# Gate sums of an mLSTM and MoE kernel: chunks 1 to 4 on 128 partitions by 128 columns, chunk 5 by itself over units 5 to 8

## The chip, the cores and the metric

The kernel runs on one core of one Trainium2 chip, as one launch. The metric is the device time of that launch in microseconds. TensorE is called PE here, VectorE DVE, ScalarE ACT, GpSimd POOL, and SyncE, which only issues DMAs in this kernel, SP.

## The reference

An mLSTM recurrence over 768 steps for 4 batches of 8 heads (head size 40), and behind it a mixture of 16 experts on the 3072 tokens that it yields. The parts that matter here are the two gates and what is derived from them:

```python
for t in range(S):                                   # S = 768
    m_new = np.maximum(f_gate[:, :, t] + m, i_gate[:, :, t])
    f_stab = np.exp(f_gate[:, :, t] + m - m_new)
    i_stab = np.exp(i_gate[:, :, t] - m_new)
    m = m_new
    C = f_stab * C + i_stab * np.einsum('bhd,bhe->bhde', vt, kt)
    n = f_stab * n + i_stab * kt
    h_tilde = np.einsum('bhde,bhe->bhd', C, qt)
    y[:, :, t] = o * h_tilde / np.maximum(np.abs(nq), 1.0)   # nq = n . q
```

Then `x = y` as 3072 rows of 320, a softmax over 4 groups and over 4 experts of the chosen group picks one expert for each token, and that expert computes `relu(x @ w1) @ w2`, weighted.

## The kernel before, in words

The sequence is cut into 6 chunks of 128 steps. A chunk of one batch is a **unit**: unit u is chunk u // 4 of batch u % 4, so units 0 to 3 are chunk 0, units 4 to 7 chunk 1, and units 20 to 23 chunk 5. Within a chunk the recurrence is written as an attention: the scores (`scores`, line 205, tile `sp`), multiplied by a decay matrix `ab` into `pt` (`masked`, line 210), times the values (`values`, line 277, tile `av`), and a state `Cflat` is carried from chunk to chunk (`carried`, line 230; `state`, line 249).

The decay matrix comes from the **gate sums**, which is what is changed. For each of the 32 heads, one running maximum M of the gates (a scan over time, line 873), the step of the decay Dl = f + M(t-1) - M(t) (lines 877 and 878), its sum A within the chunk (a scan, line 880), and i - M - A (lines 875 and 881, kept in `G`). A is split into three bf16 pieces, which stand below each other in `Apc` (32 rows each, lines 884 to 889). `aprod` (line 178) spreads them over the partitions with a matmul, and `exps` (line 188) makes `ab` from that, with a bias per column, `bcol`. `bcol`, and two more small tables with `eacol` and `decs`, come from transposes of `G` and `A_` on PE (lines 896 and 898), copied out of the accumulator by DVE (line 904), and from one matmul on the last columns of `Apc`, masked into `ends` (lines 907 and 911).

All of it is done on 32 partitions, one for each head, in three pieces that `sums` holds as generators: `gate_sums(0, P)` for chunk 0 ahead of unit 0, `gate_sums(P, 2 * P)` for chunk 1 during units 0 and 1, and `gate_sums(2 * P, S)` for chunks 2 to 5, 512 columns wide, during units 2 to 4. `sum_on(n)` advances the piece in hand by n steps (up to a `yield`), and that sets where its instructions stand in the queues. The table `(0, 0, 3, 2, 9)[u]` says how many steps follow unit u.

Up to unit 21 the order on each engine is the order in which the code is written (`tc.manual_schedule()`). A unit (`unit(u)`) issues the loads of unit u + 3 on SP, the scores of u on PE, then on DVE the normalizing of unit u - 1 (`norm1`, lines 283 to 288, and `rows`, line 293, tile `xn`), on POOL its last product (`rows2`, line 299, tile `x`), on SP the store of it to `x_d`, then `masked`, the first half of `decay(u + 2)`, the transposes of x of unit u - 1 (`turn`, line 307), `values(u)`, `state(u)` and the second half of `decay(u + 2)`. So `decay(4)`, the first unit of chunk 1, stands in unit 2, and `decay(8)`, the first of chunk 2, in unit 6. From unit 5 on the routing of tokens (`route`, lines 374 to 443) runs between units, in steps as well (`go_on`). `first_rows`, called in unit 5, fills a tile with the constants that two later steps write out as rows (lines 467 to 480); it takes a tile of the pool `wst`, which is opened once the gate tiles are given back (`gctx.close()`).

Of the kernel before, what the change touches and what calls it, by code (L numbers as in the profile page):

```python
# [58 lines left out]
def lstm_moe(ctx: ExitStack, tc: tile.TileContext, gates, qkT, nat, og, wcat, w1, w2, cst, out):  # L59
# [809 lines left out]
    def gate_sums(lo, hi):  # L869
        fg, ig = G[:, 0, lo:hi], G[:, 1, lo:hi]  # L870
        q = nc.gpsimd if lo == 0 else nc.vector
        init = NEG if lo == 0 else M_[:, lo - 1:lo]
        nc.vector.tensor_tensor_scan(M_[:, lo:hi], fg, ig, init, op0=ALU.add, op1=ALU.max)
# [3 lines left out]
        nc.vector.tensor_tensor(Dl[:, l1:hi], G[:, 0, l1:hi], M_[:, l1 - 1:hi - 1], op=ALU.add)
# [3 lines left out]
        q.tensor_tensor(Cg[:, lo:hi], Cg[:, lo:hi], A_[:, lo:hi], op=ALU.subtract)
        yield
        p0, r1, p1 = Apc[0:32, lo:hi], Dl[:, lo:hi], A1[:, lo:hi]
        nc.vector.tensor_copy(p0, A_[:, lo:hi])
        nc.vector.tensor_tensor(r1, A_[:, lo:hi], p0, op=ALU.subtract)
# [2 lines left out]
        nc.vector.tensor_tensor(Apc[64:96, lo:hi], r1, p1, op=ALU.subtract)
# [5 lines left out]
        for i in range(n):
            s = slice((cl + i) * P, (cl + i + 1) * P)
            nc.tensor.transpose(out=tp[:, 32 * i:32 * i + 32], in_=Cg[:, s], identity=ident[0:32, 0:32])
            if lo:
                nc.tensor.transpose(out=tp[:, 32 * (n + i):32 * (n + i) + 32], in_=A_[:, s], identity=ident[0:32, 0:32])
        if not lo:
            nc.vector.tensor_copy(bcol[:, 0, :], tp[:, 0:32])  # L900
            return
        w = 32 * n
        both = gp.tile([P, 2, 4 * B * H], F32, name="both")
        nc.vector.tensor_copy(both[:, :, 0:w], tp[:, 0:2 * w].rearrange("p (a w) -> p a w", a=2))
        yield
        ends = gp.tile([P, 4, B * H], BF16, name="ends")
        nc.vector.tensor_tensor(ends[:, 0:n], bc(Apc.rearrange("p (c t) -> p c t", t=P)[:, cl:ch, P - 1:P], (P, n, B * H)),
# [285 lines left out]
```

## Time and profile before

| | |
|---|---|
| three runs | 412.26, 410.71 and 407.75 us, median 410.71 us |
| profiled execution | 411.12 us, of which the span of the profile is 409.5 us |
| mean granted TensorE clock | 0.972 of full speed |
| PE busy | 387.6 us, 95% of the span |
| DVE, ACT, POOL busy | 263.9, 213.4 and 173.9 us |
| bytes by DMA | 83.38 MB, mean 204 GB/s |

The attention takes about the first 160 us of the span, the experts the rest. A row of the timeline starts with the time from the start of the span and the busy time, both in us; what stands in brackets at its end is the idle time of the engine before it and what ended that. A row of a table by stretches gives, for each engine, the busy time and the number of instructions, then the granted clock (PEclk), the share of the 16 DMA engines and GB/s.

### The profile page before, as it was taken

The numbers are of one execution on the slowest core, as the hardware profiler recorded it, in microseconds if no ns is written. First come the engines' busy times: TensorE is split into PE (matmuls) and PEld (weight loads), VectorE is DVE, ScalarE is ACT, GpSimd is POOL, SyncE is SP. The second block draws the span as 40 slices with busy tenths as digits, with TensorE's granted clock in tenths as the row PEclk, the third lists the DMA queues.
The fourth block names the chain that finished last, engine by engine and source line by source line (L and its number), as shares of the span: only waits on it lengthen the run. The fifth ranks groups of instructions, "written<-read, shape, count | busy, mean of one in ns | idle before, by whom it ended". The sixth has DMA issues, their size and how long they took to land.

```text
span 409.5 us, 9797 instructions
## 1 busy us (share of the span) xinstructions
PE 387.6 (95%) x3665; PEld 361.1 (88%) x3665; DVE 263.9 (64%) x692; ACT 213.4 (52%) x541; POOL 173.9 (42%) x232
## 2 busy tenths in 40 slices
PE   7869999999899888899999999999999999999994
PEld 4769898989778777699899999999999999999994
DVE  5695786858979795683966565765845655433530
ACT  5753555654657540534855564755745645443531
POOL 6334467666656463528524234243042325331300
PEclk9987999999999989599999999999999999999998
DMA  7934649988799953418996647676764267786700
GB/s 228 323 118 132 167 139 189 257 186 173 173 241 277 224 140 103 108 27 267 408 398 238 199 175 269 219 239 187 280 219 147 61 242 257 300 304 225 277 20 10
DMA packets 28260, 83.38 MB, mean 204 GB/s; under 512 B 11447, under 2 KB 15406, under 8 KB 24628
## 3 DMA queue, kind: packets, MB, share of 16 engines
q1 hardware_dynamic: 22756, 64.74, 53.5%
q0 software_dynamic: 5232, 17.65, 12.4%
q8 instruction: 29, 0.48, 0.5%
q10 hardware_dynamic: 224, 0.35, 0.4%
q14 instruction: 19, 0.16, 0.2%
HBM read 72.97 MB, written 9.99 MB: 203 GB/s over the span
## 4 chain that ended last, share of the span: by engine, by line
PE 69%; DMA 10%; issue 9%; DVE 5%; POOL 3%; ACT 2%; POOLq 1%; SPq 0%; ACTq 0%; DVEq 0%
PE psh L749 12%; PE av L277 9%; PE psh L717 6%; PE po L770 6%; PE po L772 6%; PE po L771 6%; PE sp L205 4%; PE it L230 3%; DMA w2s<-in_w_dram 3%; DMA x_d<-x 3%; PE it L249 2%; PE po L776 2%; PE aw L178 2%; PE tpm L307 2%; PE po L775 2%
## 5 line engine op out<-in xcount | busy, mean ns | idle before, releaser
L188 ACT ACTIVATE ab<-aw,bcol 128x128 f32<-128x128 f32 x192 | 54.5, 370 | 44.1 <-PE aw L178 43.9
L583 POOL DMA_INDIRECT out_dram<-y,ix x32 | 36.9, 1154 | 78.6 <-ACT y L782 71.3
L770 PE MATMUL po<-w2h,hh 128*128 128x320 f32 (+3 forms) x200 | 63.2, 316 | 0.9 <-ACT hh L703 0.9
L772 PE MATMUL po<-w2h,hh 128*128 128x320 f32 (+3 forms) x200 | 61.8, 309 | 0.0
L771 PE MATMUL po<-w2l,hh 128*128 128x320 f32 (+3 forms) x200 | 61.7, 309 | 0.0
L579 POOL DMA_INDIRECT xg<-x_d,ix x32 | 34.8, 1086 | 55.2 <-DMA ix<-itab 29.0
L642 DVE TENSOR_TENSOR w2l<-w2s,w2h 128x640 fp32r<-128x640 f32 x64 | 50.4, 815 | 10.6 <-ACT w2h L640 10.6
L277 PE MATMUL av<-nt,pt 128*128 128x128 f32 x384 | 50.5, 287 | 1.7 <-DVE pt L210 1.7
L277 PEld LDWEIGHTS av<-nt,pt 128*128 128x128 f32 x384 | 47.9, 202 | 2.3 <-DVE pt L210 1.9
L706 DVE SCALAR_TENSOR_TENSOR hh<-psh,hh 128x256 fp32r<-128x256 f32 (+4 forms) x108 | 35.9, 365 | 17.7 <-ACT hh L703 17.2
L703 ACT ACTIVATE hh<-psh 128x288 fp32r<-128x288 f32 (+8 forms) x68 | 30.2, 443 | 29.5 <-PE psh L749 15.0
L640 ACT CAST w2h<-w2s 128x640 fp32r<-128x640 f32 x64 | 43.2, 724 | 0.0
L717 PE MATMUL psh<-xhl,w1s 128*128 128x144 f32 (+3 forms) x336 | 41.3, 283 | 0.0
L717 PEld LDWEIGHTS psh<-xhl,w1s 128*128 128x128 f32 x336 | 40.9, 191 | 0.1
L782 ACT ACTIVATE y<-po,xg 128x320 f32<-128x320 f32 (+3 forms) x25 | 13.2, 527 | 52.1 <-PE po L772 49.7
L749 PE MATMUL psh<-xhl,w1h 128*128 128x256 f32 (+5 forms) x224 | 38.5, 294 | 0.5 <-ACT xhl L684 0.4
L210 DVE TENSOR_TENSOR pt<-sp,ab 128x512 f32<-128x512 f32 x48 | 30.9, 684 | 10.8 <-PE sp L205 9.6
L770 PEld LDWEIGHTS po<-w2h,hh 128*128 128x128 f32 (+3 forms) x200 | 36.4, 182 | 1.2 <-ACT hh L703 1.2
L772 PEld LDWEIGHTS po<-w2h,hh 128*128 128x128 f32 (+3 forms) x200 | 36.4, 182 | 0.1
L771 PEld LDWEIGHTS po<-w2l,hh 128*128 128x128 f32 (+3 forms) x200 | 36.5, 182 | 0.0
L749 PEld LDWEIGHTS psh<-xhl,w1h 128*128 128x128 f32 x224 | 32.3, 195 | 1.2 <-ACT xhl L684 0.5
L486 POOL DMA_INDIRECT itab<-tokid,slot x24 | 25.9, 1080 | 15.3 <-DVE slot L420 4.3
(195 smaller groups left out, 782.1 us busy)
## 6 DMA issues: line engine op xcount, KB each, us to landing
w1s<-in_w_dram SPq DMA_DIRECT2D x12, 1536.0 KB, 6.8
w2s<-in_w_dram SPq DMA_DIRECT2D x12, 1280.0 KB, 6.3
nt<-in_nat_dram SPq DMA_DIRECT2D x24, 324.0 KB, 6.6
qk<-in_qkT_dram SPq DMA_DIRECT2D x24, 320.0 KB, 6.1
x_d<-x SPq DMA_DIRECT2D x24, 192.0 KB, 4.5
sig<-in_og_dram SPq DMA_DIRECT2D x6, 640.0 KB, 8.1
w1s<-in_w_dram SPq DMA_DIRECT2D x4, 768.0 KB, 11.3
w1s<-in_w_dram POOLq DMA_DIRECT2D x2, 1536.0 KB, 9.1
```

The costliest lines, as they stand in the source:

```text
L188: rt["exp"] = nc.scalar.activation(st_[u]["ab"][:, r, j, :], aw[:, j, :], AF.Exp, bias=bcol[:, c, i:i + 1])
L277: ins = mm(av[:, i:i + P], t["pm"][r][:, pr, :], nt[:, o:o + P], start=True, stop=True)
L579: return nc.gpsimd.indirect_dma_start(out=o, out_offset=None, in_=src, in_offset=bass.IndirectOffsetOnAxis(ap=idx, axis=0))
L583: return nc.gpsimd.indirect_dma_start(out=out, out_offset=bass.IndirectOffsetOnAxis(ap=idx, axis=0), in_=y, in_offset=None, bounds_check=N ...
L640: nc.scalar.copy(a, src[:, s])
L642: lows.append(lambda: nc.vector.tensor_tensor(o[rows], src[rows, s], a[rows].bitcast(F32), op=ALU.subtract))
L706: nc.vector.scalar_tensor_tensor(hh[:, f:f + per, dst], src[:, :, t], 0.0, hr.bitcast(F32)[:, :, t], op0=ALU.max, op1=ALU.subtract)
L717: ins = mm(ps[:, g * W:(g + 1) * W], w1s[:, s], xhl[:, k, :], start=(k == 0), stop=(k == 2))
L749: ins = mm(ps[:, g * W:(g + 1) * W], w[:, s], x, start=(n == 0), stop=(n == len(todo) - 1))
L770: mm(po[0:m], hh[:, f, t], w2h[:, s], start=st0, stop=False)
L771: mm(po[0:m], hh[:, f, t], w2l[:, s], start=False, stop=False)
L772: ins = mm(po[0:m], hh[:, f, tl], w2h[:, s], start=False, stop=sp0)
```

## The change

The gate tiles get another shape. The inputs of the gates are laid out by chunk and head (192 rows of 2 x 128), so that rows 0 to 31 are chunk 0, rows 32 to 159 chunks 1 to 4, and rows 160 to 191 chunk 5. Chunk 0 is computed as before. Chunks 1 to 4 are one piece, `middle_sums()`, on 128 partitions (32 for each chunk) by 128 columns, where `gate_sums(P, 2 * P)` was: four scans of 32 x 128 for the running maximum, each started from the last column of the one before, which a copy moves to the next 32 partitions; everything else in single instructions of 128 x 128. The three bf16 pieces are made in `pc4`, and since `Apc` wants them on other partitions, 12 DMAs on SP's queue carry them there, one for each chunk and piece. Chunk 5 is `gate_sums(1)`, 32 x 128, taken up after unit 4 and spread over units 5 to 8 by the table `(2, 2, 1, 9)[u - 5]`. The transposes of the middle piece are two of 128 x 128, and `bcol` and `eacol` are read straight from PSUM, without the copy `both`.

```diff
+    post = enter(tc.tile_pool(name="post", bufs=2, reuse_waits="tile"))   # was opened after unit 4
...
-    G = gp.tile([B * H, 2, S], F32, name="G")
...
-    R_ = gp.tile([B * H, S], F32, name="R_")
+    G = gp.tile([BH, 2, 2, P], F32, name="G")
+    G4 = gp.tile([P, 2, P], F32, name="G4")
+    ones4 = gp.tile([P, P], F32, name="ones4")
+    M_ = gp.tile([BH, 2, P + 1], F32, name="M_")
+    M4 = gp.tile([P, P + 1], F32, name="M4")
...
+    pc4 = gp.tile([P, 3, P], BF16, name="pc4")
...
     def first_rows():
-        t = wst.tile([P, 3 * F], F32, name="w1s")
+        t = gp.tile([P, 3 * P + ROW], F32, name="rows0")
...
-    def gate_sums(lo, hi):
+    def gate_sums(g):
+        c = (NCH - 1) * g
+        fg, ig, M, dl, A = G[:, g, 0], G[:, g, 1], M_[:, g], Dl[:, g], A_[:, g]
+        q = nc.vector if g else nc.gpsimd
+        if g:
+            nc.vector.tensor_copy(M[:, 0:1], M4[P - BH:P, P:P + 1])
...                                   # the same steps on one chunk of 32 x 128
+        nc.tensor.transpose(out=tp[:, 0:BH], in_=ig, identity=ident[0:BH, 0:BH])
+        if not g:
+            nc.vector.tensor_copy(bcol[:, 0, :], tp[:, 0:BH])
+            return
+        nc.tensor.transpose(out=tp[:, BH:2 * BH], in_=A, identity=ident[0:BH, 0:BH])
+        yield from columns(tp, c, c + 1)
+
+    def columns(tp, cl, ch):
...                                   # as before, without both: ends and bcol, then the matmul, eacol, decs
+
+    def middle_sums():
+        fg, ig = G4[:, 0], G4[:, 1]
+        for k in range(NCH - 2):
+            rs = slice(k * BH, (k + 1) * BH)
+            nc.vector.tensor_copy(M4[rs, 0:1], M4[(k - 1) * BH:k * BH, P:P + 1] if k else M_[:, 0, P:P + 1])
+            nc.vector.tensor_tensor_scan(M4[rs, 1:P + 1], fg[rs], ig[rs], M4[rs, 0:1], op0=ALU.add, op1=ALU.max)
+            if k % 2:
+                yield
+        nc.vector.tensor_tensor(D4, fg, M4[:, 0:P], op=ALU.add)
+        nc.vector.tensor_tensor(D4, D4, M4[:, 1:P + 1], op=ALU.subtract)
+        yield
+        nc.vector.tensor_tensor_scan(A4, ones4, D4, 0.0, op0=ALU.mult, op1=ALU.add)
+        nc.vector.tensor_copy(pc4[:, 0], A4)
+        yield
+        nc.vector.tensor_tensor(D4, A4, pc4[:, 0], op=ALU.subtract)
+        nc.vector.tensor_copy(pc4[:, 1], D4)
+        nc.vector.tensor_tensor(pc4[:, 2], D4, pc4[:, 1], op=ALU.subtract)
+        for k in range(NCH - 2):
+            for i in range(3):
+                nc.sync.dma_start(Apc[i * BH:(i + 1) * BH, (k + 1) * P:(k + 2) * P], pc4[k * BH:(k + 1) * BH, i])
+        yield
+        nc.vector.tensor_tensor(ig, ig, M4[:, 1:P + 1], op=ALU.subtract)
+        nc.vector.tensor_tensor(ig, ig, A4, op=ALU.subtract)
+        yield
+        tp = ps_1.tile([P, 512], F32, name="tp", tag="tp")
+        nc.tensor.transpose(out=tp[:, 0:P], in_=ig, identity=ident)
+        nc.tensor.transpose(out=tp[:, P:2 * P], in_=A4, identity=ident)
+        yield from columns(tp, 1, NCH - 1)
...
-        sums.append(gate_sums(P, 2 * P))
+        sums.append(middle_sums())
...
         unit(1, first=True)
         sum_on(9)
-        sums.append(gate_sums(2 * P, S))
         for u in range(2, 5):
             unit(u)
-            sum_on((0, 0, 3, 2, 9)[u])
-    gctx.close()
+        sums.append(gate_sums(1))
+        for u in range(5, 9):
+            unit(u)
+            sum_on((2, 2, 1, 9)[u - 5])
     gctx.close()
```

How this moves rows in the queues is shown at three places. The first is SP, from the store of x of unit 0 to that of unit 1. Before:

```order
L314 DMA x_d<-x 128x384
L145 DMA qk_90<-in_qkT_dram 80x1024
L168 DMA nt<-in_nat_dram 128x648
L314 DMA x_d<-x 128x384
L145 DMA qk_91<-in_qkT_dram 80x1024
```

The same place after, where the line numbers are those of the changed file:

```order
L320 DMA x_d<-x 128x384
L941 DMA Apc<-pc_132 32x128 x12
L151 DMA qk_93<-in_qkT_dram 80x1024
L174 DMA nt<-in_nat_dram 128x648
L320 DMA x_d<-x 128x384
```

Twelve DMAs now stand between the store of unit 0 and the loads of unit 5. The kernel's DMAs share eight completion semaphores in turn, so each of them also waits until the DMA eight places ahead of it has landed.

The second place is DVE between the products of unit 1 (`pt`) and the normalizing of unit 1 (`den`). Before:

```order
L210 TENSOR_TENSOR pt<-sp,ab 128x512 x2
L884 CAST Apc<-A__122 32x128
L885 TENSOR_TENSOR Dl<-A__122,Apc 32x128
L887 CAST A_124<-Dl 32x128
L888 TENSOR_TENSOR Apc<-Dl,A_124 32x128
L904 COPY both<-tp 128x2x32
L907 TENSOR_TENSOR ends<-Apc,sel_b 128x32
L909 COPY bcol<-both 128x32
L286 TENSOR_SCALAR den<-av 128x8
```

After (`A_130` is A4, `D_129` is D4, `M_126` is M4, `pc_132` is pc4):

```order
L216 TENSOR_TENSOR pt<-sp,ab 128x512 x2
L933 SCALAR_TENSOR_TENSOR A_130<-ones_124,D_129 128x128
L934 CAST pc_132<-A_130 128x128
L936 TENSOR_TENSOR D_129<-A_130,pc_132 128x128
L937 CAST pc_132<-D_129 128x128
L938 TENSOR_TENSOR pc_132<-D_129,pc_132 128x128
L943 TENSOR_TENSOR G_123<-G_123,M_126 128x128
L944 TENSOR_TENSOR G_123<-G_123,A_130 128x128
L912 TENSOR_TENSOR ends<-Apc,sel_b 128x128
L914 COPY bcol<-tp 128x128
L292 TENSOR_SCALAR den<-av 128x8
```

`ends` reads `Apc`, which DVE and POOL wrote before; now the DMAs write it, and `ends` waits for all twelve. The row behind it is the normalizing of unit 1.

The third place is DVE in unit 2, from its products to those of unit 3. Before:

```order
L210 TENSOR_TENSOR pt<-sp,ab 128x512 x2
L873 SCALAR_TENSOR_TENSOR M__120<-G,M__120 32x512
L875 TENSOR_TENSOR G<-G,M__120 32x512
L877 TENSOR_TENSOR Dl<-G,M__120 32x512
L878 TENSOR_TENSOR Dl<-Dl,M__120 32x512
L880 SCALAR_TENSOR_TENSOR A__122<-R__123,Dl 32x512
L881 TENSOR_TENSOR G<-G,A__122 32x512
L286 TENSOR_SCALAR den<-av 128x8
```

After:

```order
L216 TENSOR_TENSOR pt<-sp,ab 128x512 x2
L292 TENSOR_SCALAR den<-av 128x8
L293 SCALAR_TENSOR_TENSOR den<-av,den 128x8
L294 RECIPROCAL den<-den 128x8
L299 SCALAR_TENSOR_TENSOR xn<-sig,av 128x320
```

The six rows of 512 columns are gone from here, and so are the four of them that stood behind the products of unit 3 and the transposes and copies behind unit 4.

More of the change, by code (lines that the diff above doesn't have):

```diff
@@ L881, in gate_sums @@
[L881 removed]
+        nc.vector.tensor_tensor_scan(A, ones4[0:BH], dl, 0.0, op0=ALU.mult, op1=ALU.add)
+        q.tensor_tensor(ig, ig, A, op=ALU.subtract)
         yield
[L883 to L885 removed]
+        p0, p1 = Apc[0:32, cols], A1[:, g]
+        nc.vector.tensor_copy(p0, A)
@@ L894, in gate_sums @@
[L894 to L907, printed above, removed]
-                                bc(sel_b.unsqueeze(1), (P, n, B * H)), op=ALU.mult)
-        nc.vector.tensor_copy(bcol[:, cl:ch, :].rearrange("p c h -> p (c h)"), both[:, 0, 0:w])
+        nc.tensor.transpose(out=tp[:, 0:BH], in_=ig, identity=ident[0:BH, 0:BH])
@@ new lines, in gate_sums @@
+        if not g:
[4 more added lines that the diff above has]
+    def columns(tp, cl, ch):
+        n = ch - cl
+        w = n * BH
+        ends = gp.tile([P, 4, BH], BF16, name="ends")
+        nc.vector.tensor_tensor(ends[:, 0:n], bc(Apc.rearrange("p (c t) -> p c t", t=P)[:, cl:ch, P - 1:P], (P, n, BH)),
+                                bc(sel_b.unsqueeze(1), (P, n, BH)), op=ALU.mult)
+        nc.vector.tensor_copy(bcol[:, cl:ch, :].rearrange("p c h -> p (c h)"), tp[:, 0:w])
@@ L924, in lstm_moe @@
     with tc.manual_schedule():
-        nc.sync.dma_start(G[:, :, 0:P], gates[:, :, 0:P])
+        nc.sync.dma_start(G[:, 0], gates[0:BH])
         nc.scalar.dma_start(cs, cst)
-        nc.scalar.dma_start(G[:, :, P:], gates[:, :, P:])
+        nc.scalar.dma_start(G4, gates[BH:BH + P])
+        nc.scalar.dma_start(G[:, 1], gates[BH + P:])
         nc.vector.memset(ones_b, 1.0)
@@ L931, in lstm_moe @@
         busy(11)
[L932 to L934 removed]
+        nc.vector.memset(ones4, 1.0)
+        nc.vector.memset(Dl[:, 0, 0:1], 0.0)
         nc.vector.memset(Apc[96:P], 0.0)
@@ L986, in lstm_moe @@
     mxp = enter(tc.tile_pool(name="mxp", bufs=2, reuse_waits="tile"))
-    post = enter(tc.tile_pool(name="post", bufs=2, reuse_waits="tile"))
     pools["ws"] = [wsa]
@@ L991, in lstm_moe @@
     with tc.manual_schedule():
-        for u in range(5, MANUAL):
+        for u in range(9, MANUAL):
             unit(u, 6 if 13 <= u <= 16 else 0)
@@ L1136, in _lay @@
     q, k, v, o = (inputs[n] for n in ('q', 'k', 'v', 'o_gate'))
-    gates = c(np.stack([inputs['f_gate'].reshape(B * H, S), inputs['i_gate'].reshape(B * H, S)], axis=1))
+    gates = np.stack([inputs['f_gate'].reshape(B * H, NCH, P), inputs['i_gate'].reshape(B * H, NCH, P)], axis=2)
+    gates = c(gates.transpose(1, 0, 2, 3).reshape(NCH * B * H, 2, P))
     def tr(a):
```

43 lines of the change are left out of this document (19 added, 24 removed).

## The prediction

> **What bounds the kernel now.** I read the shares of busy time first, then the granted clock, then a table with one stretch for each unit of the attention.
>
> ```profile
> PE 387.6 (95%) x3665; PEld 361.1 (88%) x3665; DVE 263.9 (64%) x692; ACT 213.4 (52%) x541; POOL 173.9 (42%) x232
> PEclk9987999999999989599999999999999999999998
> ```
>
> PE is busy for 95%, so what counts is where PE stands still or runs at a lower clock. The clock falls once early, in the slices from about 20 to 41 us, which are units 2 to 4. The stretches below run from the first scores of one unit to those of the next: units 1, 2, 3, 4, 5, 6, 7, 8 and 9.
>
> ```profile
> 12.47:20.03 7.56, 6.35 (x79) 5.24 (x75) 3.89 (x16) 5.09 (x20) 2.86 (x8) 1.00 1.05 335
> 20.03:24.96 4.93, 4.68 (x60) 4.11 (x60) 4.62 (x10) 2.52 (x11) 1.42 (x2) 1.00 0.57 179
> 24.96:35.27 10.31, 7.34 (x62) 6.57 (x60) 9.02 (x20) 3.97 (x11) 3.89 (x5) 0.68 0.31 86
> 35.27:41.48 6.21, 6.21 (x100) 5.62 (x100) 3.20 (x9) 2.97 (x11) 2.68 (x5) 0.99 0.46 142
> 41.48:49.14 7.66, 7.05 (x87) 6.13 (x86) 5.20 (x16) 3.60 (x14) 3.65 (x6) 1.00 0.65 196
> 49.14:54.95 5.81, 5.81 (x88) 5.41 (x86) 4.49 (x17) 3.05 (x11) 2.92 (x5) 1.00 0.65 186
> 54.95:60.77 5.82, 5.66 (x78) 5.09 (x76) 5.33 (x14) 3.95 (x11) 5.01 (x7) 1.00 0.30 92
> 60.77:67.49 6.72, 6.66 (x103) 5.77 (x101) 4.28 (x13) 3.43 (x13) 4.42 (x8) 1.00 0.81 107
> 67.49:72.90 5.41, 5.41 (x78) 5.02 (x77) 3.83 (x12) 2.50 (x10) 3.63 (x6) 1.00 1.13 258
> ```
>
> Unit 2 takes 4.93 us and unit 3, with the same work on PE, 10.31 us. Unit 5 takes 7.66 us, where its like, unit 9, takes 5.41. Elsewhere PE is full. The timeline and the clock show what happens in unit 3:
>
> ```profile
> 22.50 1.26 DVE L873 TENSOR_TENSOR_SCAN M__120<-G,M__120 32x512 f32<-32x512 f32 x1
> 27.07 0.68 DVE L881 TENSOR_TENSOR G<-G,A__122 32x512 f32<-32x512 f32 x1
> 27.68 0.15 DVE L286 TENSOR_SCALAR den<-av 128x8 f32<-128x8 f32 x1
> 29.47 0.90 PE L307 MATMUL tp<-cs,x 128*128 128x128 f32 x3 [2.83 <-POOL x L299]
> 30.17 3.62 PE L277 MATMUL av<-nt,pt 128*128 128x128 f32 x16
> 28.00:28.50 0.50, 0.00 (x0) 0.00 (x0) 0.47 (x3) 0.00 (x0) 0.00 (x0) 1.00 0.00 0
> 28.50:29.00 0.50, 0.00 (x0) 0.00 (x0) 0.50 (x3) 0.00 (x0) 0.30 (x1) 0.60 0.00 0
> 35.00:35.50 0.50, 0.50 (x6) 0.30 (x5) 0.17 (x1) 0.12 (x1) 0.50 (x1) 0.57 0.00 0
> ```
>
> From 22.50 to 27.68 us DVE does the six instructions of 512 columns, the normalizing of unit 2 waits behind them, and PE stands still for 2.83 us until x of that unit is there. Then the clock is at half from about 28.7 to 35.3 us.
>
> **What goes.** Without the wide instructions unit 3 should cost what unit 2 does: 10.31 - 4.93 = **5.4 us** gained, idle time and low clock together. Units 4 and 5 together take 13.87 us, units 8 and 9 12.13; so without the eight transposes and the wait for `ends` in unit 5, **1.7 us** gained. That is 7.1 us in all, and the most that the change can bring.
>
> **What comes between units 1 and 2.** The rows there, and small instructions for prices:
>
> ```profile
> 3.56 0.41 DVE L873 TENSOR_TENSOR_SCAN M__120<-G 32x128 f32<-32x128 f32 x1 [0.90 <-DMA G<-in_gates_dram]
> 4.00 0.28 DVE L877 TENSOR_TENSOR Dl<-G,M__120 32x127 f32<-32x127 f32 x1
> 9.92 1.05 DVE L873 TENSOR_TENSOR_SCAN M__120<-G,M__120 32x128 f32<-32x128 f32 x1
> 9.97 0.72 POOL L217 TENSOR_TENSOR kw<-nt,ab 128x320 f32<-128x320 f32 x1
> 12.50 0.15 DVE L286 TENSOR_SCALAR den<-av 128x8 f32<-128x8 f32 x1
> 12.68 0.17 DVE L287 SCALAR_TENSOR_TENSOR den<-av,den 128x8 f32<-128x8 f32 x1
> 14.87 0.30 DVE L884 CAST Apc<-A__122 32x128 bf16<-32x128 f32 x1
> 15.20 0.28 DVE L885 TENSOR_TENSOR Dl<-A__122,Apc 32x128 f32<-32x128 f32 x1
> 16.52 0.74 POOL L217 TENSOR_TENSOR kw<-nt,ab 128x320 f32<-128x320 f32 x1 [1.43 <-DVE Apc L888]
> 19.68 0.18 DVE L907 TENSOR_TENSOR ends<-Apc,sel_b 128x32 bf16<-128x32 bf16 x1
> 19.92 0.18 PE L911 MATMUL tp<-ends,ones_b 128*128 128x32 bf16 x1 [0.41 <-DVE ends L907]
> 20.03 1.16 PE L205 MATMUL sp<-qk 64*128 64x128 f32 x16
> 143.22 0.48 DVE L299 TENSOR_TENSOR x<-xn,den 128x320 f32<-128x320 f32 x1
> ```
>
> A scan of 128 columns costs 0.44 us from start to start (3.56 to 4.00). A copy of one column isn't in the trace; the nearest are rows of 8 columns, 0.18 us from start to start (12.50 to 12.68), and nothing at all is the other end. Four copies and scans: 4 x 0.62 = 2.5 us, and two subtractions of 128 columns at 0.3, 0.6 us. That 128 partitions cost no more than 32 I read from the last row: 128 x 320 in 0.48 us lies halfway between 32 x 128 in 0.28 (line 885) and 32 x 512 in 0.68 (line 881), as 320 does between 128 and 512. With the 0.64 us that the scan at 9.92 lost beside POOL's product (1.05 against 0.41), DVE reaches the normalizing of unit 0 at 9.92 + 3.8 = 13.7 us, 1.2 later than 12.50. PE doesn't feel that: it needs the products of unit 1 only at 16 us. They end near 16.1; then a scan (0.44) and a cast (0.33, 14.87 to 15.20) make the first piece. POOL's product at 16.52 falls on them, for up to 0.74 us. So SP can issue the first of the 12 DMAs at 16.9 to 18.3 us; I take **17.6**.
>
> The prices of such DMAs:
>
> ```profile
> L479 SPq DMA_DIRECT2D x_d<-w1s x4: 428/443/478, 66.5 to 67.9; - x4
> 68.85 0.24 SPq L480 DMA_DIRECT2D x_d<-w1s  x1
> 69.19 0.35 SPq L152 DMA_DIRECT2D sig<-in_og_dram  x1
> 1.74 0.56 SPq L145 DMA_DIRECT2D qk<-in_qkT_dram  x1
> 5.01 0.42 SPq L168 DMA_DIRECT2D nt<-in_nat_dram  x1
> 0.95 0.73 SPq L925 DMA_DIRECT2D G<-in_gates_dram  x1
> DMA to landing us min/median/max: 2.0/4.5/11.6
> ```
>
> Issues one behind the other cost 0.45 us each (line 479), at best 0.34 (68.85 to 69.19), at worst 0.55 (1.74 to 5.01 in six steps). No DMA from SBUF to SBUF is in the trace. The gates' own 32 KB took from 0.95 to 3.56, 2.6 us, and the stores of x (last line) between 2.0 and, at the median, 4.5. I take 2.3 from issue to landing, near the small one, since by 20 us the first loads are through: the share of the DMA engines falls from 1.05 in unit 1 to 0.57 in unit 2. The last of the twelve lands at 17.6 + 11 x 0.45 + 2.3 = 24.9 us. `ends` waits for it on DVE, and PE's matmul for `ends`; from `ends` to the scores took 0.35 us (19.68 to 20.03), with four times the columns 0.45. The scores of unit 2 start at 25.3 in place of 20.03: **5.3 us** lost. Queued behind `ends` are the normalizing and the products of unit 2; behind PE's matmul, all of unit 2. Loads of unit 5 go behind the twelve on SP, which is hidden: unit 5 is 15 us away.
>
> PE then stands still from about 19.8 to 25.2 us, longer than the 2.83 us that brought the half clock in unit 3. I let it cost the same as there, where the values alone took 3.62 us: 10.31 - 2.83 - 4.93 = **2.5 us** for the clock; bounds 0 (no fall) and 3. The Trainium skill, TensorE: Matmul & The Clock Gate, section "What's actually happening", lets the clock fall after one idle window of about 3.4 us and come back after one busy window of 3.4 us. Here it fell 2 us after PE's last work and took nearly 6 us of work to come back, so the trace differs; by the page's window the loss would be about 1.6 us and the sum 412.5.
>
> **What comes in units 5 to 8.** Chunk 5 costs DVE a copy and a scan (0.62 us) and three subtractions (0.9) behind unit 5, a scan and three narrow ones (1.3) behind unit 6, two (0.5) behind unit 7 and two (0.4) in unit 8: 3.8 us. DVE is busy for 4.49 of 5.81 us in unit 6 and for 5.33 of 5.82 in unit 7, so part of that will push the normalizing, then x, then PE's transposes of x. Bounds 0 and 3.8 us; I take **1.3**, because each unit has about 0.5 to 1.3 us of room on DVE and a third of the sum goes past it. Two transposes and a matmul on PE in unit 8: **0.3** (three at about 0.1).
>
> **The sum.** -5.4 - 1.7 + 5.3 + 2.5 + 1.3 + 0.3 = +2.3 us on the profiled execution's 411.1 (span 409.5 and 1.6 around it): **413.4**. That execution lies 0.4 us above the median 410.7. The moved constants and the early opening of `post` cost nothing: POOL has idle time in every unit. ACT's third load of gates at the start delays its first casts by 0.7 us at most, over a microsecond before PE needs them.
>
> **Rivals.**
> - *Transfers nearly hidden.* Issues at 0.34, landing 2.0, first piece at 16.9: scores of unit 2 at 23.0, +3.0; clock 1.5, units 5 to 8 nothing: 411.1 + 3.0 + 1.5 + 0.3 - 7.1 = 408.8, and 407.3 if the clock doesn't fall. For it: 0.34 is a measured step. Against it: it needs all the low ends together. Chance 0.16.
> - *DVE becomes the bound in units 5 to 8 (slower side).* Beside its 3.8 us, each unit's gate instructions can stand still beside one of POOL's products, as the scan at 9.92 did (0.64 us). It decides once a unit's extra passes the room, which in unit 7 is 0.49 us. 3.8 + 4 x 0.7 = 6.6 us against some 2 us of room: 4.6 in place of 1.3, so 416.7. The Trainium skill, SBUF — State Buffer, section "Who interferes with whom", says that a DVE instruction with two inputs in SBUF and a GpSimd instruction that reads SBUF exclude each other; the trace agrees (1.05 against 0.41 us). Chance 0.15.
> - *Late landing.* The twelve queue behind loads still in flight, or wait on their eight semaphores: 4.5 us to landing, scores at 27.5, +7.5, clock 3: 416.1. For it: the DMA engines are full (1.05) in all of unit 1. Chance 0.12.
> - *The shift is swallowed.* If a later wait for transfers set the time whatever the attention does, 411.1. For it, a row of the chain of waits, behind unit 16:
>
> ```profile
> 124.19 12.89 DMA w2s<-in_w_dram
> ```
>
>   Against it: those transfers are released by the routing of earlier units and would shift with them. Chance 0.12.
>
> **How the numbers follow.** The forecast itself has 0.45. The range 408.5 to 418 takes in the rivals and leaves out the joint extremes. About 1% is what a measurement of this kernel can tell from no change: 4.1 us. Faster by more than that needs the first rival with a clock that stays up, or gains I don't see: 0.10. Slower by more: most of the second and third rivals and a small part of the forecast, 0.30. The rest, 0.60.
>
> **What would show it.** In the changed profile: unit 3 near 5 us and unit 5 near 5.5; an idle PE of about 5 us before the matmul on `ends`, released by DVE, which itself waits for a DMA into `Apc`; twelve issues on SP about 0.45 us apart from 17.6 us; a half clock for some 6 us from about 22 us on; units 6 to 8 together about 1 us longer than 18.35. Wrong it would be if DVE's wait for `Apc` were under 3 us, or units 6 to 8 unchanged.

## The result, and the profile after

The changed kernel takes 415.31 us, the median of four runs (414.58 to 416.31); the kernel before, in four runs beside it, 410.13 us (407.75 to 412.26). The ratio is 1.013, with a 95% interval from 1.009 to 1.017: slower by a little over 1%. The forecast was 413.4 us, 2.3 above the profiled execution of before. The profiled execution took 414.86 us, of which the span is 413.3; before, 411.12 and 409.5.

First the busy share and the granted clock, from the page of the changed kernel:

```profile
PE 387.8 (94%) x3659; PEld 361.3 (87%) x3659; DVE 259.3 (63%) x697; ACT 213.3 (52%) x541; POOL 173.1 (42%) x231
PEclk9968999999999998779999999999999999999999
```

PE does the same work, 387.8 us in place of 387.6, in a span that is 3.8 us longer. The early dip of the clock is there still. A table by stretches, again with one row for each of units 1 to 9, shows where the time went:

```profile
12.28:26.99 14.71, 6.51 (x79) 5.22 (x75) 6.73 (x22) 5.51 (x21) 2.66 (x7) 0.87 0.58 169
26.99:34.48 7.49, 7.49 (x60) 6.90 (x59) 2.40 (x8) 2.35 (x9) 1.41 (x2) 0.57 0.38 125
34.48:39.40 4.92, 4.78 (x62) 4.19 (x60) 2.80 (x10) 3.85 (x11) 2.50 (x3) 1.00 0.54 147
39.40:45.93 6.53, 6.47 (x102) 5.70 (x100) 3.78 (x11) 3.31 (x13) 3.35 (x5) 1.00 0.55 168
45.93:51.29 5.36, 5.36 (x76) 4.96 (x75) 3.84 (x12) 2.51 (x10) 3.28 (x6) 1.00 0.84 269
51.29:58.43 7.14, 6.00 (x88) 5.41 (x86) 6.34 (x24) 3.05 (x11) 4.10 (x6) 1.00 0.50 153
58.43:64.46 6.03, 5.63 (x77) 5.04 (x76) 5.56 (x19) 3.94 (x11) 4.20 (x7) 1.00 0.70 94
64.46:70.69 6.23, 6.23 (x102) 5.64 (x100) 4.19 (x14) 3.08 (x11) 3.96 (x7) 1.00 0.71 124
70.69:77.28 6.59, 6.59 (x82) 5.77 (x80) 4.10 (x14) 3.40 (x14) 3.97 (x6) 1.00 1.07 297
```

Set against the stretches of before, this gives the account by terms (us; plus is time lost):

| term | forecast | measured | from |
|---|---|---|---|
| scores of unit 2 start later | +5.3 | +6.96 | 26.99 against 20.03 |
| unit 2, half clock | +2.5 | +2.56 | 7.49 against 4.93 |
| unit 3 | -5.4 | -5.39 | 4.92 against 10.31 |
| units 4 and 5 | -1.7 | -1.98 | 6.53 + 5.36 against 13.87 |
| units 6 to 9 | +1.6 | +2.28 | 25.99 against 23.71 |
| sum | +2.3 | +4.43 | 77.28 against 72.85 |

By the start of unit 10 the kernel is 4.4 us behind, and it is 4.4 us behind at unit 22 too (151.11 against 146.68). Up to there nothing takes it back. By the profiled executions the whole costs 3.7 us and by the medians 5.2; single executions scatter by more than the difference between these.

The first term is read from SP's twelve issues, and from DVE and PE behind them. The first two lines answer for all instructions of line 941; the others are rows of the timeline:

```profile
L941 SPq DMA_DIRECT2D Apc<-pc x12: 532/588/630, 17.2 to 24.2; - x12
DMA to landing us min/median/max: 1.7/1.8/3.7
26.25 0.29 DVE L912 TENSOR_TENSOR ends<-Apc,sel_b 128x128 bf16<-128x128 bf16 x1 [7.61 <-DMA Apc<-pc]
26.46 0.28 DVE L914 COPY bcol<-tp 128x128 f32<-128x128 f32 x1
26.79 0.26 PE L916 MATMUL tp<-ends,ones_b 128*128 128x128 bf16 x1 [7.41 <-DVE bcol L914]
26.99 2.08 PE L211 MATMUL sp<-qk 64*128 64x128 f32 x16
```

The twelve start between 17.2 and 24.2 us, 0.63 us apart (7.0 / 11), though an issue itself lasts 0.59. `ends` starts 2.0 us after the last issue. PE waits 7.41 us, and the releaser named is `bcol`, which stands behind `ends` on DVE. So from `ends` to the scores it takes 0.74 us.

The clock, in four stretches of 1 us (the third number from the end of a row):

```profile
22.00:23.00 1.00, 0.00 (x0) 0.00 (x0) 0.00 (x0) 0.00 (x0) 0.00 (x0) 1.00 0.06 12
23.00:24.00 1.00, 0.00 (x0) 0.00 (x0) 0.00 (x0) 0.00 (x0) 0.00 (x0) 0.59 0.06 12
32.00:33.00 1.00, 1.00 (x6) 1.00 (x6) 0.00 (x0) 0.00 (x0) 0.00 (x0) 0.50 0.00 0
33.00:34.00 1.00, 1.00 (x20) 0.85 (x18) 0.00 (x0) 0.00 (x0) 0.00 (x0) 0.79 0.00 0
```

PE's last work ends at 19.4 us, the clock falls at 23.2, and it is whole again at 33.4.

Units 6 and 9 show where chunk 5 costs time. Rows of the timeline, DVE and PE around the start of unit 6, then PE at the start of unit 9:

```profile
50.41 0.14 DVE L881 COPY M__125<-M 32x1 f32<-32x1 f32 x1
51.82 0.49 DVE L289 TENSOR_TENSOR av<-av,num 128x328 f32<-128x328 f32 x1
53.22 0.32 DVE L270 TENSOR_TENSOR Cflat<-Cflat,it 128x164 f32<-128x164 f32 x1
53.59 1.16 PE L236 MATMUL it<-Cflat,qk 64*128 64x128 f32 x16 [1.14 <-DVE Cflat L270]
70.69 0.48 PE L211 MATMUL sp<-qk 64*128 64x128 f32 x2
71.36 0.24 PE L901 MATMUL tp<-cs,G 32*128 32x32 f32 x1
72.03 0.19 PE L916 MATMUL tp<-ends,ones_b 128*128 128x32 bf16 x1
```

In unit 6 the gate rows of chunk 5 run from 50.41 us until the normalizing of unit 5 starts at 51.82; the update of the state `Cflat` stands behind that, and PE's product with the state (`carried`) waits 1.14 us for it. In unit 9 the two transposes of chunk 5 (one is shown) and its matmul on `ends` stand between the scores, which start at 70.69 and are cut twice.

### The profile page after: what moved, and what is told of

It reads as the page before. It is cut to its first block, busy times and chain, and to the rows that moved or that the text cites. A ratio compares the mean times of both kernels' runs of the same rounds, so it can differ in the third digit from the quotient of the medians.

```text
span 413.3 us, 9806 instructions
## 1 busy us (share of the span) xinstructions
PE 387.8 (94%) x3659; PEld 361.3 (87%) x3659; DVE 259.3 (63%) x697; ACT 213.3 (52%) x541; POOL 173.1 (42%) x231
## 4 chain that ended last, share of the span: by engine, by line
PE 71%; DVE 13%; issue 8%; ACT 2%; DMA 2%; SPq 1%; POOLq 1%; POOL 1%; DVEq 0%; ACTq 0%
PE psh L755 13%; PE av L283 8%; PE psh L723 6%; PE po L776 5%; PE po L777 5%; PE po L778 5%; PE it L236 4%; PE sp L211 4%; PE tpm L313 2%; PE po L782 2%; PE aw L184 2%; PE po L781 2%; PE busy L127 2%; PE it L255 2%; DMA w1s<-in_w_dram 2%
## 5 line engine op out<-in xcount | busy, mean ns | idle before, releaser
L305 POOL TENSOR_TENSOR x<-xn,den 128x320 f32<-128x320 f32 x20 | 14.3, 716 | 47.8 <-DVE xn L299 46.7
```

## The experiments

All times of a unit are read from the starts of its scores. Those repeat well: unit 3 takes 4.91 or 4.92 us in every kernel here that doesn't do the wide gate rows in it. Total times of one kernel scatter by over 1%, so a difference of 1 us is read from the units. The theory was that SP's price for each issue sets the wait, that the wait brings the half clock, and that chunk 5's rows hold up the state's update. The first rival was that the transfers themselves are slow or wait for others.

**No DMAs: twelve copies on DVE.**

```diff
-                nc.sync.dma_start(Apc[i * BH:(i + 1) * BH, ...], pc4[k * BH:(k + 1) * BH, i])
+                nc.vector.tensor_copy(Apc[i * BH:(i + 1) * BH, ...], pc4[k * BH:(k + 1) * BH, i])
```

> The changed kernel with the twelve DMAs into Apc replaced by twelve DVE copies of 32 x 128. Theory (the loss is SP's twelve issues at 0.63 us each, then one landing): the copies cost DVE about 12 x 0.2 = 2.5 us, the scores of unit 2 start near 22 us in place of 26.99, PE stands still for about 2.8 us; 415.3 - 4.8 = 410.5 us if the clock still falls (unit 2 near 7.5 us), near 408 if it stays up (unit 2 near 5). Rival (something else holds the scores of unit 2, such as DVE's own work or loads in flight): they start at 26 us or later, and the time stays within 1 us of 415.3.

The copies' row of the timeline and the stretch of unit 2:

```profile
17.77 2.36 DVE L941 COPY Apc<-pc 32x128 bf16<-32x128 bf16 x12
21.80:27.86 6.06, 6.06 (x60) 5.51 (x59) 2.83 (x10) 2.35 (x9) 1.41 (x2) 0.72 0.33 109
```

Twelve copies take 2.36 us, 0.2 us each, where twelve DMAs take 9.0 from the first issue to the last landing. The scores of unit 2 start at 21.80 us, 5.2 earlier. The total is 409.02 us, a ratio of 0.997 (0.993 to 1.001) to the kernel before: the loss is gone, and it came with the DMAs.

**The tables of chunk 1 first.** Those of chunks 2 to 4 go behind unit 4, so that only three of the twelve DMAs are waited for at unit 2.

```diff
-        yield from columns(tp, 1, NCH - 1)
+        yield from columns(tp, 1, 2, 0, P)
+
+    def middle_columns():
...
+        yield from columns(tp, 2, NCH - 1, BH, P + BH)
```

> The changed kernel with the small tables (ends, bcol, eacol, decs) of chunk 1 alone behind unit 1, and those of chunks 2 to 4 behind unit 4; all twelve DMAs stay, in the same order, those of chunk 1 first. Theory (issue count): three issues end by 18.5 us and land by 20.5, the scores of unit 2 start near 21, PE's idle time is under 2 us and the clock stays up, unit 2 takes 5 us; the second set of tables costs 1.3 to 1.9 us in unit 5; 415.3 - 5.9 - 2.5 + 1.5 = 408.4 us. Rival (the landing of such a DMA is what is slow, however many there are): scores not before 25 us, and about 415 us.

```profile
22.17 0.19 DVE L914 TENSOR_TENSOR ends<-Apc,sel_b 128x32 bf16<-128x32 bf16 x1 [3.25 <-DMA Apc<-pc]
```

The scores of unit 2 start at 22.62 us, later than the 21 expected. The third issue starts near 18.8 us, and `ends` only at 22.17: the DMAs issued early take over 3 us to land, those issued late 1.8, so cutting twelve to three saves less than nine times 0.63. The clock was expected to stay up and fell: unit 2 takes 6.07 us. The ratio is 1.002 (0.999 to 1.005).

**Work for PE during the wait.** 26 matmuls whose result nobody reads, ahead of the matmul on `ends`.

```diff
+        busy(26)
         yield from columns(tp, 1, NCH - 1)
```

> The changed kernel with 26 matmuls on constants that nobody reads, put on PE between the transposes and the matmul on ends, where PE stands still. Theory (unit 2 is long because the clock falls): granted clock 1.00 throughout units 1 to 3, scores of unit 2 still near 27 us, unit 2 near 5.0 us in place of 7.49, so 415.3 - 2.5 = 412.8 us. Rival (unit 2 is long because its data come late): the clock stays up, and unit 2 takes 7 us or more all the same, 415 us.

```profile
12.34:26.99 14.65, 12.22 (x103) 7.75 (x100) 6.66 (x22) 5.52 (x21) 2.65 (x7) 1.00 0.50 157
26.99:31.91 4.92, 4.89 (x61) 4.14 (x60) 2.46 (x8) 2.36 (x9) 1.42 (x2) 1.00 0.67 207
```

The scores of unit 2 start at 26.99 us, as in the changed kernel, but the clock stays whole and unit 2 takes 4.92 us in place of 7.49. So the second term is 2.57 us, and it is the clock's. The total, 412.29 us (ratio 1.008, 1.004 to 1.012), is 3 us below the changed kernel's.

**What an issue costs by its form.** The kernel before, with sixteen small DMAs that nobody waits for (four of each form, 32 partitions by 256 bytes in the first three), in places where SP has nothing else to do.

```diff
+                nc.sync.dma_start(scr[a, 0:P], scs[a])                                 # SBUF, same partitions
+                nc.sync.dma_start(scr[a, P:2 * P], scs[96 - 32 * j:128 - 32 * j])      # SBUF, moved
+                nc.sync.dma_start(scf[a], gates[:, 0, 64 * j:64 * j + 64])             # from HBM, 32 partitions
+                nc.sync.dma_start(scg[:, 64 * j:64 * j + 64], cst[:, 64 * j:64 * j + 64])   # from HBM, 128
```

> The kernel before, with sixteen DMAs added to SP's queue that nobody reads: behind the loads of unit 3 four of 32 x 256 bytes within SBUF on the same partitions and four that move to other partitions, behind those of unit 4 four of 32 x 256 bytes from HBM, behind those of unit 5 four of 128 x 256 bytes from HBM. Theory (an issue within SBUF is dearer by its form): 0.59 us for both kinds within SBUF, 0.45 or less for those from HBM. Rival (0.59 us belonged to the place, with the first loads still in flight and the waits on eight semaphores): 0.45 us for all four kinds.

SP's rows of the timeline, four issues each:

```profile
25.40 3.13 SPq L150 DMA_DIRECT2D scr<-scs  x4
28.58 2.50 SPq L152 DMA_DIRECT2D scr<-scs  x4
34.29 1.82 SPq L154 DMA_DIRECT2D scf<-in_gates_dram  x4
40.85 1.85 SPq L156 DMA_DIRECT2D scg<-in_cst_dram  x4
```

From SBUF to SBUF an issue costs 0.62 us with moved partitions; with the same partitions the mean is 0.78, because one of the four took 1.23, and the others lasted 0.59 as the moved ones did. From HBM it is 0.46, with 32 partitions as with 128. The four forms stand at different places, but loads in flight don't explain the difference: the mean busy share of the DMA engines was 0.09 during the moved ones and 0.66 and 0.91 during those from HBM. The 0.45 us of the prediction was right for the form that it was read from, and wrong for this one.

**Two queues.** The last four DMAs are issued by ACT.

```diff
+                q = nc.scalar if k == NCH - 3 or (k, i) == (NCH - 4, 2) else nc.sync
+                q.dma_start(Apc[i * BH:(i + 1) * BH, ...], pc4[k * BH:(k + 1) * BH, i])
```

> The last four of the twelve DMAs into Apc are issued by ACT instead of SP. Theory (each DMA costs its queue 0.63 us to issue, and nothing else is slow): SP issues eight from 17.2 to 22.2 us, ACT four from about 20.3 us, when its last exponentials of unit 3 end, to 22.7; the last lands 1.8 us behind its issue, near 24.0; scores of unit 2 at about 24.5 in place of 26.99, total about 2.5 us below the changed kernel's 414.9, unit 2 still about 7.3 us long for the clock. Rival (the DMAs into Apc are slow themselves, one behind the other in the DMA engines, whoever issues them): scores of unit 2 stay at 26.5 to 27, total within 0.5 us of the changed kernel.

Rows of SP, ACT and DVE:

```profile
16.94 6.74 SPq L942 DMA_DIRECT2D Apc<-pc  x8
22.17 2.52 ACTq L942 DMA_DIRECT2D Apc<-pc  x4
27.61 0.29 DVE L912 TENSOR_TENSOR ends<-Apc,sel_b 128x128 bf16<-128x128 bf16 x1 [9.26 <-DMA nt<-in_nat_dram]
```

A miss: the scores start at 28.35 us, later than with one queue, and the total of this one execution is 416.76 us. ACT's four begin at 22.17 and not at 20.3, for a reason that the trace doesn't name, and SP too stands still for 1.6 us between its sixth and seventh issue; the trace names the store of x as what SP waited for. And SP, which is now sooner done with its eight, puts the loads of unit 5 into the DMA engines at 23.78, ahead of ACT's last issue at 24.1; the trace lets DVE's wait end with them, though `ends` doesn't read what they bring. On ACT an issue costs 0.63 us too (2.52 for four). Whether fewer issues on SP shorten the wait is not tested by this run, since other things make the wait: issues held back on both queues, and the loads. That the rival's number (26.5 to 27) was nearer is no support for it either.

**Eight DMAs, and four.** The cleaner test: fewer DMAs on the same queue, the rest copied by DVE, which has nothing to do there. With `i == 2` DVE takes the third pieces (eight DMAs are left), with `i > 0` two of three (four are left).

```diff
+                if i == 2:
+                    nc.vector.tensor_copy(Apc[i * BH:(i + 1) * BH, ...], pc4[k * BH:(k + 1) * BH, i])
+                    continue
                 nc.sync.dma_start(Apc[i * BH:(i + 1) * BH, ...], pc4[k * BH:(k + 1) * BH, i])
```

> Eight DMAs into Apc instead of twelve: the third pieces of chunks 1 to 4 are copied by DVE, which stands idle there in the changed kernel. Theory (SP's 0.63 us for each issue sets the end of the wait): first issue 17.2, the eighth at 17.2 + 7 x 0.63 = 21.6, landing 1.8 to 2.0 later, ends and the matmul 0.7 behind it: scores of unit 2 at 24.1 to 24.4, 2.5 us ahead of the changed kernel's 26.99; unit 2 still 6 to 7.5 us long for the clock; units 3 to 9 as in the changed kernel. Rival (the transfers themselves are slow, or the last of them waits for loads in flight): scores at 26 us or later, since the first eight of the changed kernel then land no sooner.

> Four DMAs into Apc, the first pieces; DVE copies the other eight. Theory (SP's 0.63 us for each issue): the fourth issue at 17.2 + 3 x 0.63 = 19.1; landing 1.8 us, or 3.7 us for one that is issued while the loads are in flight, so 20.9 to 22.8; scores of unit 2 at 21.6 to 23.5, and by the three DMAs of the split tables (landed 22.2) near the upper end, so the step from eight to four DMAs gives less than 2.5 us. Rival (the transfers are slow themselves): 25 us or later.

SP's issues and the row of `ends` with eight, then with four:

```profile
17.26 5.05 SPq L944 DMA_DIRECT2D Apc<-pc  x8
23.50 0.29 DVE L912 TENSOR_TENSOR ends<-Apc,sel_b 128x128 bf16<-128x128 bf16 x1 [3.91 <-DMA Apc<-pc]
```

```profile
16.95 2.52 SPq L944 DMA_DIRECT2D Apc<-pc  x4
21.25 0.29 DVE L912 TENSOR_TENSOR ends<-Apc,sel_b 128x128 bf16<-128x128 bf16 x1 [1.30 <-DMA Apc<-pc]
```

With eight, the scores of unit 2 start at 24.25 us, in the middle of the forecast 24.1 to 24.4; with four at 21.94, inside 21.6 to 23.5. `ends` starts at 26.25, 23.50 and 21.25 us with twelve, eight and four: 0.69 and 0.56 us for each DMA left out, with the first issue at 17.23, 17.26 and 16.95. The wait grows with the number of issues on SP and is over 1.8 to 2.4 us after the last of them starts. Slow transfers don't make it: the time to landing is 1.8 us at the median of the twelve and longest, 3.7, at the first, so nothing piles up behind the queue, and the issue alone sets the pace. One execution each: 411.96 and 409.01 us.

**Chunk 5 earlier.** Its sums behind units 2 and 3; its tables stay behind unit 8.

```diff
-        for u in range(2, 5):
-            unit(u)
         sums.append(gate_sums(1))
-        for u in range(5, 9):
+        for u in range(2, 9):
             unit(u)
-            sum_on((2, 2, 1, 9)[u - 5])
+            sum_on({2: 3, 3: 2, 8: 9}.get(u, 0))
```

> The gate sums of chunk 5 stand behind units 2 and 3, where DVE has room, instead of behind units 5 to 7; their transposes and small tables stay behind unit 8. Theory (units 6 to 8 are longer because the gate rows stand ahead of the state's update on DVE, and unit 9 because the tables cut into its scores): unit 6 back from 7.14 to about 5.8 us, unit 7 from 6.03 to 5.8, unit 8 stays near 6.3, unit 9 stays near 6.6; units 6 to 9 about 1.5 us shorter, total about 413.4. Units 2 and 3 grow by less than 0.5 us. Rival (units 6 to 9 are longer for another reason, such as the moved loads or the early opening of the pool post): unit 6 stays near 7.1 us and the total at 414.9. Second rival (the rows cost as much wherever they stand): units 2 and 3 grow by the 1.5 us that units 6 and 7 lose.

The stretches of units 2, 6 and 7:

```profile
27.22:33.33 6.11, 6.11 (x60) 5.55 (x59) 4.48 (x16) 2.35 (x9) 1.42 (x2) 0.71 0.51 160
50.15:55.96 5.81, 5.81 (x88) 5.41 (x86) 4.50 (x17) 3.06 (x11) 2.92 (x5) 1.00 0.66 186
55.96:62.08 6.12, 5.65 (x77) 5.08 (x75) 5.64 (x14) 3.96 (x11) 5.01 (x7) 1.00 0.31 90
```

Unit 6 is back at 5.81 us, which is what it took before, so the 1.33 us there were chunk 5's rows on DVE. Unit 7, expected at 5.8, takes 6.12, with 0.47 us of waiting for x. Units 8 and 9 take 6.34 and 6.59, as in the changed kernel: what they lose goes with the tables. Unit 2 holds seven gate rows more on DVE, and PE is still full in it; it is even shorter than the changed kernel's, because the clock came back sooner. Second rival excluded: the same rows cost nothing where DVE has room. The total is 413.94 us, ratio 1.007 (1.004 to 1.010).

**Both together.** Chunk 1's tables first, chunk 5's sums behind units 2 and 3, and the tables of chunks 2 to 5 together behind unit 4. The lines are set against the version with chunk 1's tables first.

```diff
-        sums.append(middle_columns())
+        sums.append(gate_sums(1))
         for u in range(2, 5):
             unit(u)
-            sum_on((0, 0, 0, 0, 9)[u])
+            sum_on({2: 3, 3: 9}.get(u, 0))
+            if u == 3:
+                sums.append(middle_columns())    # now columns(tp, 2, NCH, ...)
+            if u == 4:
+                sum_on(9)
```

> Tables of chunk 1 alone behind unit 1, so that only three DMAs are waited for; sums of chunk 5 behind units 2 and 3; the tables of chunks 2 to 5 together behind unit 4. Theory: scores of unit 2 at about 22.6 us as when the tables were split alone; units 6 to 9 back to 5.8, 5.8, 6.3 and 5.4 us, about 1.7 to 2.3 us below the split alone; unit 5 longer by up to 0.5 us for two more transposes; profiled execution about 406.5. Rival (the shift is swallowed by a later wait for transfers): 408.5 as with the split alone, though the units are shorter.

Unit 2 starts at 22.20 us, units 6 to 9 take 5.81, 5.44, 6.25 and 6.03, and unit 10 starts at 70.99, 1.7 us ahead of the split alone (72.67), at the low end of the forecast. The end doesn't show it: 408.94 us in the profiled execution against 408.46, ratio 0.999 (0.995 to 1.003). Unit 22, here and then in the split alone, shows where it went:

```profile
144.98:153.16 8.18, 6.82 (x61) 6.40 (x59) 6.97 (x20) 2.48 (x7) 5.88 (x12) 0.82 0.12 28
146.51:153.34 6.83, 5.48 (x61) 5.07 (x59) 6.03 (x20) 2.48 (x7) 5.99 (x12) 1.00 0.14 34
```

At its start this version is still 1.53 us ahead. In it the clock falls at 150.29 us, in the other profile not, and unit 22 takes 1.35 us longer. The kernel before and the changed one have the same fall there (unit 22 takes 8.47 and 8.28 us), three other versions have not (6.83 or 6.84). So in this pair of profiles it was the clock that swallowed the gain, and not, as the rival had it, a wait for transfers.

**Chunk 1 by engine copies.** As the last one, but chunk 1's three pieces are carried by DVE, POOL and DVE; the other nine DMAs have till unit 4.

```diff
+                if k == 0:
+                    (nc.vector, nc.gpsimd, nc.vector)[i].tensor_copy(Apc[i * BH:(i + 1) * BH, P:2 * P], pc4[0:BH, i])
+                else:
                     nc.sync.dma_start(...)
```

> As the split with the early sums of chunk 5, and chunk 1's three pieces are carried into Apc by two copies on DVE and one on POOL instead of three DMAs; the other nine DMAs have till unit 4. Theory (the wait for the DMAs at unit 2 is what the change loses by, and the low clock behind it): nothing is waited for at unit 2, its scores start at 20.0 to 20.7 us as before the change, the clock stays at 1.00 through units 2 to 4, unit 2 takes 4.9 us and unit 3 4.9; 2.0 to 2.6 us below the split with the early sums; profiled execution about 404.5, some 1.3% below the kernel before. Rival (the low clock comes from something else than PE standing still for the tables): unit 2 or 3 still loses 1 us or more to a lower clock, and the total is 406 or more.

The stretches of units 2, 4 and 5, and the first product of unit 5 with the state:

```profile
20.01:24.93 4.92, 4.78 (x61) 4.14 (x60) 4.35 (x14) 2.36 (x11) 1.42 (x2) 1.00 0.20 58
29.85:37.70 7.85, 7.41 (x107) 6.26 (x105) 3.37 (x8) 4.18 (x15) 2.94 (x4) 1.00 0.68 186
37.70:45.34 7.64, 7.21 (x76) 6.55 (x75) 5.22 (x18) 2.35 (x9) 3.63 (x6) 0.78 0.45 148
39.29 1.51 PE L236 MATMUL it<-Cflat,qk 64*128 64x128 f32 x16 [0.43 <-DVE Cflat L270]
```

Unit 2 starts at 20.01 us, where it started before the change, and takes 4.92, as does unit 3. The kernel is faster than the one before: 406.57 us, ratio 0.988 (0.984 to 0.992). But unit 5 takes 7.64 us at a clock of 0.78. PE stands still for 0.38 us for `bcol` and 0.43 us for the state, which wait behind each other on DVE, and here the clock falls for that. In the version before it, with the same two waits, it did not (unit 5: 6.06 us). The clock changes only at the borders of windows of 3.41 us (the table further below). Here both waits lie in one window, from 36.54 to 39.95 us; there a border, at 41.05, cuts the first wait in two (40.87 to 41.25), so that no window holds both. That this made the difference is likely, but one pair of profiles doesn't show it.

**`bcol` by ACT.** As the last one; the copy out of PSUM goes to ACT, behind the matmul on `ends`.

```diff
-        nc.vector.tensor_copy(bcol[:, cl:ch, :]..., tp[:, tb:tb + w])
-        yield
         mm(tp[:, te:te + w], ones_b, ends[:, 0:n]..., start=True, stop=True)
+        nc.scalar.copy(bcol[:, cl:ch, :]..., tp[:, tb:tb + w])
```

> As the version with chunk 1 carried by engine copies, and bcol is copied out of PSUM by ACT instead of DVE, behind the matmul on ends, so that neither DVE nor PE waits for the transposes in unit 4. Theory (in that version PE stood still for 0.38 and 0.43 us around the tables of chunks 2 to 5, because DVE's normalizing of unit 4 stood behind its copy of bcol, and the clock fell to half from 40 to 43 us for it): unit 4 takes about 7.4 us in place of 7.85, unit 5 5.4 in place of 7.64, the clock stays at 1.00 till unit 9; 2.7 us gained, the median about 404, 1.7% below the kernel before. Rival (the clock falls there because PE's work is thin, not because it stands still): unit 5 stays above 7 us, the median at 406.

The stretches of units 2 to 5:

```profile
19.42:24.34 4.92, 4.91 (x62) 4.14 (x60) 3.97 (x12) 3.15 (x14) 1.42 (x2) 1.00 0.11 22
24.34:29.25 4.91, 4.77 (x61) 4.22 (x59) 4.41 (x14) 3.85 (x11) 2.83 (x4) 1.00 0.97 317
29.25:36.67 7.42, 7.36 (x107) 6.26 (x106) 4.51 (x12) 4.19 (x15) 3.66 (x5) 1.00 0.75 229
36.67:42.03 5.36, 5.36 (x76) 4.97 (x75) 3.78 (x12) 2.52 (x10) 2.96 (x5) 1.00 0.64 214
```

PE is busy for at least 97% of each of them, the clock stays whole, and units 4 and 5 take 7.42 and 5.36 us as forecast. Unit 10 starts at 65.54 us, 7.3 ahead of the kernel before. The median is 403.61 us, ratio 0.988 (0.983 to 0.992): faster than the kernel before and the changed one, and by the interval not told apart from the version ahead of it, though 3.5 us of the attention lie between the two profiles.

**The changed kernel again.** A second profile of the same program, for what repeats.

> The changed kernel itself, a second profiled execution. Theory (the clock is set by windows of 3.41 us whose phase has nothing to do with the program): the starts of units and their lengths repeat within 0.1 us wherever the clock is whole, the scores of unit 2 start at 26.9 to 27.1 again, but the clock falls at another moment, between 22.8 and 26.2 us, and the half clock lasts another whole number of times 3.41 us or the same one with other edges; unit 2 takes anything from 6.0 to 7.6 us. Rival (the clock follows the program's own idle time at a fixed distance): it falls at 23.2 and returns at 33.4 us again, within 0.2 us, and unit 2 takes 7.49 us.

The scores of unit 2 start at 27.03 us (26.99 the first time), units 3, 4 and 5 take 4.91, 6.54 and 5.36, and unit 6 takes 7.14 again. The clock fell at 22.64 us and was whole at 32.89: both edges 0.54 us earlier relative to the program, and the same distance between them. Unit 2 took 7.22 us. The fall lies just outside the stretch that the theory expected, and farther from 23.2 than the rival allowed, so this pair alone decides little; the next table decides it.

## Why the prediction was right and where it was off

The sign, the places and the mechanism held: 413.4 us was forecast, 415.31 came, inside the range. By unit 10 the loss was 4.4 us, where the sum gave 2.3. Point by point, by its own steps:

- **What goes.** Unit 3 fell to 4.92 us, by 5.39 for a forecast of 5.4; units 4 and 5 gained 1.98 for 1.7. A unit's like, without the work in question, was a good price for it.
- **DVE ahead of unit 1.** Copies of one column cost 0.18 us from start to start, the scans 0.48 (the first of the four 0.83), the instructions on 128 partitions 0.29 as on 32; the normalizing of unit 0 starts at 13.88 us (forecast 13.7), and PE doesn't feel it.
- **The term that was too small: the price of an issue.** The working took 0.45 us from stores of another form, with 0.55 as the worst. It is 0.63 from SBUF to SBUF, so that the eleven steps cost 7.0 us and not 5.0: 2.0 us, which is nearly all of the miss in the sum (4.43 against 2.3), and PE stood still for 7.41 us and not for about 5. The other parts of that term nearly offset each other, which is luck: the first issue came at 17.23 (17.6 forecast), the landing took 2.0 (2.3), and from `ends` to the scores it was 0.74 (0.45), as PE also waits for `bcol`.
- **The clock.** 2.5 us was forecast, 2.56 came, and the matmuls without a reader took 2.57 back. The size was right, partly by luck, and the reading of the trace behind it was not: the half clock lasted 10.25 us and not some 6, in the second profile of the same program it cost 2.30 us (7.22 against 4.92), and with chunk 5 early 1.19 after the same wait. The prediction said that the trace differs from the window of about 3.4 us that the Trainium skill, TensorE: Matmul & The Clock Gate, section "What's actually happening", gives. Read in stretches of 0.125 us, the half clock lasted as follows. The last two columns have the next fall in the same profile, and its distance from the first one in units of 3.4136 us (the 133.13 us of the changed kernel, divided by 39):

| profile | half clock from, to (us) | lasted | next fall | distance |
|---|---|---|---|---|
| before | 28.60, 35.43 | 6.83 | 151.48 | 36.00 |
| changed | 23.18, 33.43 | 10.25 | 156.31 | 39.00 |
| changed, again | 22.64, 32.89 | 10.25 | 155.77 | 39.00 |
| copies | 22.04, 25.45 | 3.41 | 148.33 | 37.00 |
| split | 23.54, 26.96 | 3.42 | 163.49 | 41.00 |
| two queues | 21.09, 34.73 | 13.64 | 157.62 | 40.00 |
| eight DMAs | 22.68, 29.52 | 6.84 | 152.40 | 38.00 |
| four DMAs | 23.66, 27.07 | 3.41 | 47.55 | 7.00 |
| chunk 5 early | 23.93, 30.75 | 6.82 | 153.64 | 38.00 |
| both | 23.99, 27.40 | 3.41 | 150.29 | 37.00 |
| engine copies | 39.96, 43.36 | 3.40 | 159.42 | 35.00 |

  The two falls of the changed kernel, in the rows that they are read from (a clock of 0.73 in a stretch of 0.125 us is half clock in its last 0.07 us):

```profile
23.12:23.25 0.12, 0.00 (x0) 0.00 (x0) 0.00 (x0) 0.00 (x0) 0.00 (x0) 0.73 0.00 0
156.25:156.38 0.12, 0.12 (x2) 0.11 (x1) 0.12 (x2) 0.12 (x1) 0.10 (x2) 0.71 0.00 0
```

  Each half clock lasted a whole number of times 3.41 us, and within a profile the next fall lies a whole number of such windows behind the first, over up to 140 us of quite different work. So the windows run through on their own: the program doesn't start them, and in another execution they lie elsewhere in it, as the two profiles of the changed kernel show. The window that the Trainium skill gives is there; the "nearly 6 us of work" that the prediction saw were a first window that still held idle time and a second one that didn't. In the changed kernel one window held no work, the next one 0.2 us of idle time, and the third was full; so work ran at half clock in two of them, and the 1.6 us that one would have cost were too little.
- **Units 6 to 9.** 1.6 us was forecast, 2.28 came, and by a path that the prediction didn't name: not x and its transposes, but the state's update behind the same rows, for which PE waited 1.14 us in unit 6 and 0.40 in unit 7. The running of chunk 5 in units 2 and 3 gave back 1.24 of the 1.54 us of units 6 and 7. Units 8 and 9 lose 0.74 us together (12.82 against 12.08; the prediction's 12.13 took the start of unit 10 0.05 us late), where 0.3 was put: with the tables elsewhere ("both together") they take 12.28, so about 0.5 of it is the tables.
- **The rivals.** Nearly hidden transfers were excluded by the issue price. The bound on DVE came in unit 6, where DVE is busy for 6.34 of 7.14 us, but without the price that the rival put on POOL's products: none of the gate rows of chunk 5 took over 0.47 us. Late landing is real, 3 us and more, but for the first two or three DMAs alone, where it isn't what is waited for in the changed kernel. Nothing swallowed the shift up to unit 22.

## What to carry to other kernels

A small piece that only has to change partitions is carried by an engine's copy in 0.2 us, while a DMA from SBUF to SBUF costs its queue 0.63 and lands 2 us later; DMAs are for pieces that nobody needs soon. A narrower shape of the work (four scans of 128 for one of 512) gains what it promises, 7.4 us here, and the gain is kept only if its results reach their readers without a wait: the version with copies for chunk 1, chunk 5 where DVE has room and `bcol` on ACT starts unit 10 at 65.54 us where this change started it at 77.28. When a price is read from the nearest row, its form (from where to where) counts for more than its size. And before two profiles are compared by their ends, the granted clock is compared along the way: one fall of it was worth 1.1 to 2.6 us here, and whether it came differed between versions whose work at that place is the same.
